# Retention by 64x64 blocks on quarters of TensorE's array, with decays as powers of the position and the state summed in PSUM

## The chip, the cores and the metric

The kernel runs on one core of a Trainium2 chip. The metric is the time of one execution on the device, in microseconds; lower is better. TensorE multiplies matrices and writes its sums to PSUM, VectorE (DVE), ScalarE (ACT) and GpSimd (POOL) do elementwise work, and SyncE (SP) issues the transfers between device memory and the on-chip memory SBUF. Each engine works through its own queue in order.

## The reference

For each of 8 batch rows and 8 heads, retention over 576 positions with head size 64, then two feed-forward layers over all 4608 tokens. Everything is in 32-bit floats.

```python
scores = (1 / sqrt(64)) * (q @ k.T)                     # per head, 576 x 576
ret = scores * where(i >= j, gamma[h] ** (i - j), 0)    # gamma[h] = 1 - 2 ** (-5 - h)
x = (ret @ v)                                           # heads side by side: 4608 x 512
x = square(relu(x @ moe_w_in)) @ moe_w_out              # 512 -> 2048 -> 512
y = elu(x @ moe2_w_in) @ moe2_w_out                     # 512 -> 2048 -> 512
```

## The kernel before

Tokens are cut into 9 blocks of 512 (`TB`). The first projection of the first layer (`up`, L393-403) goes block by block and, within a block, over 16 slices `f` of 128 features: per slice 12 matmuls of 512 columns, since weights and activations are each split into a high and a low half and three of the four products are kept. `act` (L414) applies relu and square on ScalarE and stores the result to device memory (`gd`). The other three projections follow later (from about 567 us) with seven products of a Strassen scheme in place of eight; `up_product` and `Down.multiply` (L570, L722) are their matmuls. The change does not touch them except for `m_tile`, which says in which of two pools a tile of theirs lies.

Retention makes the activations of the first projection. It is done in 40 chunks (`CHUNKS`): every batch row has four chunks of 128 positions and one of 64, the short one last in even batch rows and first in odd ones, so that no chunk crosses a block. For chunk `c`, with `s` its first position and `n` its length, and head pairs `p` (4) of heads `e` (2):

- `a_load` (L292) loads q and k with the head dimension on partitions, and k and v with positions on partitions.
- `a_scores` (L304): k times q, one matmul per head with 64 rows of the array, 128 columns of output positions.
- `a_decay` (L315): VectorE multiplies the scores by a table of scaled decays, zero above the diagonal.
- `a_qscale` and `a_kscale` (L324, L330): q and k are scaled by powers of gamma; on VectorE inside the loop, on GpSimd at the start.
- `a_out` (L337): the running state times the scaled q (one matmul per head pair, since the state holds two heads as diagonal blocks of a 128x128 matrix), plus v times the decayed scores, summed in one PSUM tile `o`.
- `a_evac` (L353): ScalarE copies `o` to `xraw`.
- `a_state` (L363): VectorE scales the state by a power of gamma, TensorE forms k times v in PSUM (`d`), VectorE adds it to the state.

Four chunks are worked off at the start, for block 0. The chunks of block n+1 are inserted between the slices of block n: a table `at` gives the steps, and at such a step `second(c)` (output, copy-out, state) and `first(c+1)` (scores, scalings, decay of the next) are issued just before the 12 matmuls of the slice; the loads of chunk c+2 are issued right after. `x_split` near the end of a block splits the finished activations into halves.

Two further strands run beside. In block 0, `Converter` turns the weights from 64-bit to 32-bit floats (`join` on VectorE) and splits them (`Half`), one half-slice per step. From block 1 on, `factor_steps` (L250) prepares the weight factors of the later Strassen products: 48 `Factors`, each with three steps spread over the loop: load of raw weights, conversion, sums on VectorE (L225), and a split in two (`split`, L227): ScalarE writes the high half to a tile of its own, GpSimd writes the low half in place; `store` (L237) writes each with one transfer to device memory (`wd`), the previous factor's at the start of the next. High and low halves use a ring of five tiles (`turn`). The order inside the first block is left to the tile framework's order of issue; later it is written out.

Of the kernel before, what the change touches and what calls it, by code (L numbers as in the profile page):

```python
# [51 lines left out]
C_D, C_Q, C_G, C_K = 0, 1024, 1536, 1544  # L52
C_W = 1664
# [3 lines left out]

def constants():
# [4 lines left out]
    i = np.arange(128)  # L63
    rel = i[None, :] - i[:, None]
    for h in range(H):
        p, e = divmod(h, 2)
        dec = np.where(rel >= 0, scale * gamma[h] ** np.maximum(rel, 0), 0.0)
        t[:, C_D + (e * NP + p) * 128:][:, :128] = dec
        t[64 * e:64 * e + 64, C_Q + p * 128:C_Q + p * 128 + 128] = scale * gamma[h] ** i
        t[64 * e:64 * e + 64, C_G + p] = gamma[h] ** 128  # L70
        t[64 * e:64 * e + 64, C_G + NP + p] = gamma[h] ** 64
        t[:, C_K + h] = gamma[h] ** (128 - i)
        t[:64, C_K + H + h] = gamma[h] ** (64 - i[:64])
    return t.astype(np.float32)
# [3 lines left out]
def retention_moe_moe(ctx, tc, qk_full, qk_half, kv, w1, w2, cst, out):  # L78
# [107 lines left out]
    turns = [0]  # L186

    def turn(shape, dtype, name):
        n = turns[0] % 5
        turns[0] += 1  # L190
        if n > 2:
            return place(23 + n, shape, dtype, name)
        return mpool.tile(shape, dtype, tag=f"turn{n}", name=name)

    class Factors:
# [13 lines left out]
        def start(self):  # L209
            self.r = turn([128, 8, 128], F32, "qr")  # L210
# [16 lines left out]
        def split(self):  # L227
# [3 lines left out]
            h = turn([128, 7, 128], F32R, "qh")  # L231
            nc.scalar.activation(out=h, in_=r, func=ACTF.Copy)  # L232
# [40 lines left out]
    decay = cs[:, C_D:C_D + 1024].rearrange("p (e q i) -> p e q i", e=2, q=NP)  # L273
    qdec = cs[:, C_Q:C_Q + 512].rearrange("p (q i) -> p q i", q=NP)
# [88 lines left out]
    def a_state(c, eng):  # L363
        b, s, n = CHUNKS[c]
        kv_c = kv_t.pop(c)
        if s + n == S:
            return
# [605 lines left out]
```

## Time and profile before

| | |
|---|---|
| median of 3 runs | 1636.27 us (1635.28 to 1638.92) |
| profiled execution | 1638.09 us, its span 1636.0 us |
| mean granted TensorE clock | 0.992 |
| first projection begins | 33.55 us after the span's start |
| later stages begin | about 567 us |
| TensorE busy | 1599.3 us (98%) |
| VectorE, ScalarE, GpSimd busy | 1247.2, 883.5, 133.0 us |
| moved by DMA | 379 MB |

The profile is of one execution. A group's line gives the line of the kernel, the engine, the operation, the tiles written and read, their shapes, how many there were, the busy time in us and the mean length of one in ns, and then how long the engine stood idle before them and what ended that. Matmuls overlap, so their lengths are not their cost; the distance from start to start is. TensorE's weight loads have rows of their own (PEld). "DMA share" is the share of the time in which the 16 DMA engines worked, and "PEclk" the share of the full clock that TensorE was granted.

### The profile page before, as it was taken

The numbers are of one execution on the slowest core, as the hardware profiler recorded it, in microseconds if no ns is written. First come the engines' busy times: TensorE is split into PE (matmuls) and PEld (weight loads), VectorE is DVE, ScalarE is ACT, GpSimd is POOL, SyncE is SP. The second block draws the span as 40 slices with busy tenths as digits, with TensorE's granted clock in tenths as the row PEclk, the third lists the DMA queues.
The fourth block names the chain that finished last, engine by engine and source line by source line (L and its number), as shares of the span: only waits on it lengthen the run. The fifth ranks groups of instructions, "written<-read, shape, count | busy, mean of one in ns | idle before, by whom it ended". The sixth has DMA issues, their size and how long they took to land. (4 is left out here: it accounts for less than half of the span.)

```text
span 1636.0 us, 25789 instructions
## 1 busy us (share of the span) xinstructions
PE 1599.3 (98%) x9832; PEld 1497.8 (92%) x9832; DVE 1247.2 (76%) x1580; ACT 883.5 (54%) x1207; POOL 133.0 (8%) x75
## 2 busy tenths in 40 slices
PE   7999999999999999999999999999999999999998
PEld 6887787787888899999999999999999899999998
DVE  7948667676757188899889688888888877776875
ACT  3555455455556544554454577777777544444443
POOL 3312222222222000000000000000000000000000
PEclk8999999999999999999999999999999999999999
DMA  7869999889988993653577984644658864345241
GB/s 253 270 188 317 304 286 309 278 266 327 305 283 270 317 379 137 249 200 135 206 247 244 343 311 181 215 182 153 222 202 307 329 237 134 98 155 163 89 136 39
DMA packets 230683, 378.99 MB, mean 232 GB/s; under 512 B 15776, under 2 KB 169376, under 8 KB 230560
## 3 DMA queue, kind: packets, MB, share of 16 engines
q1 hardware_dynamic: 230560, 377.35, 68.4%
q8 instruction: 77, 1.26, 0.3%
q14 instruction: 46, 0.38, 0.1%
HBM read 220.00 MB, written 157.29 MB: 231 GB/s over the span
## 5 line engine op out<-in xcount | busy, mean ns | idle before, releaser
L703 ACT ACTIVATE gh<-gq 128x768 fp32r<-128x768 f32 x336 | 284.7, 848 | 371.4 <-PE w L722 150.8
L709 DVE TENSOR_TENSOR gl<-gq,gh 128x768 fp32r<-128x768 f32 x336 | 316.8, 954 | 147.4 <-ACT gh L703 147.3
L722 PE MATMUL w<-gh,wf 128*128 128x384 f32 x1152 | 292.5, 334 | 0.0
L399 PE MATMUL h<-xp,w 128*128 128x512 f32 x576 | 230.8, 401 | 2.5 <-ACT r L418 1.7
L401 PE MATMUL h<-xp,w 128*128 128x512 f32 x576 | 226.3, 393 | 3.4 <-DVE xp L388 3.4
L400 PE MATMUL h<-xp,w 128*128 128x512 f32 x576 | 226.4, 393 | 0.0
L722 PEld LDWEIGHTS w<-gh,wf 128*128 128x128 f32 x1152 | 208.1, 188 | 0.0
L722 PE MATMUL a<-gh,wf 128*128 128x384 f32 x768 | 195.0, 334 | 1.5 <-ACT gh L703 1.5
L722 PE MATMUL e<-gh,wf 128*128 128x384 f32 x768 | 195.1, 334 | 0.0
L722 PE MATMUL w<-gl,wf 128*128 128x384 f32 x576 | 192.8, 335 | 0.2 <-DVE gl L709 0.2
L694 DVE TENSOR_TENSOR gq<-gq 128x1536 f32<-128x1536 f32 x96 | 168.5, 1755 | 1.7
L570 PE MATMUL w<-xc,wf 128*128 128x384 f32 x864 | 161.4, 334 | 0.0
L570 PEld LDWEIGHTS w<-xc,wf 128*128 128x128 f32 x864 | 150.8, 188 | 0.0
L722 PEld LDWEIGHTS a<-gh,wf 128*128 128x128 f32 x768 | 138.6, 188 | 1.9 <-ACT gh L703 1.8
L722 PEld LDWEIGHTS e<-gh,wf 128*128 128x128 f32 x768 | 138.8, 188 | 0.0
L399 PEld LDWEIGHTS h<-xp,w 128*128 128x128 f32 x576 | 109.5, 190 | 29.2 <-ACT r L418 2.2
L401 PEld LDWEIGHTS h<-xp,w 128*128 128x128 f32 x576 | 109.0, 189 | 28.7 <-DVE xp L388 5.1
L234 POOL TENSOR_TENSOR qr<-qr,qh 128x896 fp32r<-128x896 f32 x48 | 102.3, 2131 | 347.1 <-ACT qh L232 259.4
L722 PE MATMUL a<-gl,wf 128*128 128x384 f32 x384 | 128.5, 335 | 1.7 <-DVE gl L709 1.7
L722 PE MATMUL e<-gl,wf 128*128 128x384 f32 x384 | 129.4, 337 | 0.0
L400 PEld LDWEIGHTS h<-xp,w 128*128 128x128 f32 x576 | 109.4, 190 | 21.8
L418 ACT ACTIVATE r<-h 128x512 f32<-128x512 f32 x144 | 84.9, 590 | 77.6 <-PE h L401 77.1
(81 smaller groups left out, 2337.1 us busy)
## 6 DMA issues: line engine op xcount, KB each, us to landing
gq<-gd SPq DMA_DIRECT2D x96, 768.0 KB, 5.8
wf<-wd SPq DMA_DIRECT2D x84, 512.0 KB, 6.6
gd<-h SPq DMA_DIRECT2D x96, 384.0 KB, 3.3
qraw<-w SPq DMA_DIRECT2D x96, 256.0 KB, 4.8
xc<-x2d SPq DMA_DIRECT2D x30, 768.0 KB, 6.6
wd<-qh SPq DMA_DIRECT2D x48, 448.0 KB, 4.8
wd<-qr SPq DMA_DIRECT2D x48, 448.0 KB, 5.0
gd<-g SPq DMA_DIRECT2D x96, 192.0 KB, 3.6
```

What stands on the lines that cost most here:

```text
L234: nc.gpsimd.tensor_tensor(out=rl, in0=r, in1=h.bitcast(F32), op=ALU.subtract)
L399: nc.tensor.matmul(out=h, lhsT=w[:, 0, k, :], rhs=x[k][:, 0, :], start=(k == 0), stop=False)
L400: nc.tensor.matmul(out=h, lhsT=w[:, 1, k, :], rhs=x[k][:, 0, :], start=False, stop=False)
L401: nc.tensor.matmul(out=h, lhsT=w[:, 0, k, :], rhs=x[k][:, 1, :], start=False, stop=(k == KC - 1))
L418: nc.scalar.activation(out=r, in_=h, func=ACTF.Relu)
L570: nc.tensor.matmul(out=t[:, jj, :TP], lhsT=w[:, jj, c, a, :], rhs=x[:, b, c, :], start=(i in FRESH and c == 0 and n == 0), stop=(c == 1 an ...
L694: nc.vector.tensor_tensor(out=gq[out, h], in0=gq[x, h], in1=gq[y, h], op=op)
L703: nc.scalar.activation(out=gh, in_=src, func=ACTF.Copy)
L709: nc.vector.tensor_tensor(out=gl, in0=src, in1=gh.bitcast(F32), op=ALU.subtract)
L722: nc.tensor.matmul(out=t[:, c, :TP], lhsT=w[:, jj, c, a, :], rhs=parts[b][:, jj, :], start=(i in FRESH and q == 0 and jj == 0 and m == 0), ...
```

## The change

gamma^(i-j) is written as gamma^(i-256) times gamma^(256-j), with positions counted in the batch row. v is multiplied by the second factor once (`a_vscale`, VectorE; GpSimd for the later chunks at the start), and the finished output by the first, in the copy-out (`a_evac`), which moves from ScalarE to VectorE. So scores need only a mask of ones and zeros, q and k are not scaled, and k times v needs no decay: its sum over the chunks of a batch row stays in one PSUM tile (`d_t`), and ScalarE copies that to `state` after each chunk (`a_state`).

Scores are computed for 64x64 blocks, with 64 rows and 64 columns of the array to each matmul, and the block above the diagonal is left out. Heads of odd pairs have their position halves swapped on partitions. State times q, per head, also takes a quarter of the array, for which half of the heads of q are loaded a second time on the other partitions (`q2`). p times v takes quarters for the first 64 output positions and all 128 rows for the second 64; the next chunk's scores are issued between these two (`insert`). Chunks are loaded three ahead in place of two, k one later than the rest. The large table `fall` of position powers is loaded whole at the start. `o` has one buffer of two banks.

In `Factors`, the raw tile `qr` has two fixed places, and both halves go into one tile `hl`, alternating by 128 elements, with two buffers; one transfer stores both. `m_tile` puts tile 5 into the second pool.

```diff
-C_D, C_Q, C_G, C_K = 0, 1024, 1536, 1544
-C_W = 1664
+C_M, C_V, C_G = 0, 192, 272
+C_W = C_G + KC * S
...
+    mask = np.ones((2, 64, 3, 64))
+    mask[0, :, 0], mask[1, :, 0], mask[1, :, 1], mask[0, :, 2] = (causal,) * 4
...
+            t[:, C_V + H * c + h] = gamma[h] ** (256 - (s + j))
...
+            t[64 * half:64 * half + 64, C_G + S * k:C_G + S * k + S] = \
+                scale * gamma[2 * p + e] ** (np.arange(S) - 256)
...
-            self.r = turn([128, 8, 128], F32, "qr")
+            self.r = place(26 + self.n % 2, [128, 8, 128], F32, "qr")
...
-            h = turn([128, 7, 128], F32R, "qh")
-            nc.scalar.activation(out=h, in_=r, func=ACTF.Copy)
-            rl = self.r.bitcast(F32R)[:, at:at + 7, :]
-            nc.gpsimd.tensor_tensor(out=rl, in0=r, in1=h.bitcast(F32), op=ALU.subtract)
-            self.halves = (h.bitcast(F32), rl.bitcast(F32))
+            self.hl = mpool.tile([128, 7, 2, 128], F32R, tag="hl", name="hl", bufs=2)
+            nc.scalar.activation(out=self.hl[:, :, 0, :], in_=r, func=ACTF.Copy)
+            nc.gpsimd.tensor_tensor(out=self.hl[:, :, 1, :], in0=r,
+                                    in1=self.hl[:, :, 0, :].bitcast(F32), op=ALU.subtract)
...
-            for n, half in enumerate(self.halves):
-                nc.sync.dma_start(out=wd[self.layer, part][:, :, q, jj, c, n, :], in_=half)
+            nc.sync.dma_start(out=wd[self.layer, part][:, :, q, jj, c, :, :], in_=self.hl.bitcast(F32))
...
+    mask = cs[:, C_M:C_M + 192].rearrange("p (g i) -> p g i", g=3)
+    grow = cs[:, C_V:C_V + 10 * H].rearrange("p (c h) -> p c h", c=10)
+    fall = cs[:, C_G:].rearrange("p (w e t) -> p w e t", w=2, e=2)
+    state = apool.tile([128, 2, 2, D], F32, name="state")
...
-        t = apool.tile([128, 2, NP, n], F32, tag="qk", name="qk", bufs=2)
+        if c % 3:
+            t = place(23 + c % 3, [128, 2, NP, n], F32, "qk")
+        else:
...
-        t = apool.tile([128, 2, H, D], F32, tag="kv", name="kv", bufs=2)
-        nc.sync.dma_start(out=t[:n], in_=kv[b * S + s:b * S + s + n])
-        kv_t[c] = t
+        if s:
+            q2_t[c] = ring.tile([128, 2, n], F32, tag=f"t{2 + c % 3}", name="q2")
+            src = q2_full[FULL.index(c)] if n == 128 else q2_half[HALF.index(c)]
+            nc.sync.dma_start(out=q2_t[c], in_=src)
+        if c % 3:
+            v = apool.tile([128, H, D], F32, tag="v", name="v", bufs=2)
+        else:
+            v = ring.tile([128, H, D], F32, tag="t5", name="v")
+        nc.sync.dma_start(out=v, in_=kv[c, :, 1])
+        v_t[c] = v
+
+    def k_load(c):
+
+        b, s, n = CHUNKS[c]
+        if s + n < S:
+            k_t[c] = apool.tile([128, H, D], F32, tag="k", name="k", bufs=2)
+            nc.sync.dma_start(out=k_t[c], in_=kv[c, :, 0])
+
...
-        for p in range(NP):
-            for e, sc in enumerate(sc_t[c]):
-                r = slice(64 * e, 64 * e + 64)
-                nc.tensor.matmul(out=sc[:n, p, :n], lhsT=qk[r, 1, p, :], rhs=qk[r, 0, p, :],
-                                 start=True, stop=True)
+        for pp in range(2):
+            for half in range(n // 64):
+                for p in range(2 * pp, 2 * pp + 2):
+                    for e, sc in enumerate(sc_t[c]):
+                        r = slice(64 * e, 64 * e + 64)
+                        to = slice(64 * ((half + p) % 2), 64 * ((half + p) % 2) + 64)
+                        k = qk[r, 1, p, 64 * half:64 * half + 64]
+                        if half == 0 and p % 2 == 0:
+                            q, out = qk[r, 0, p, :], sc[to, pp, :n // 64, :]
+                        elif half == 0 and n == 128:
+                            q = qk[r, 0, p, :].rearrange("p (g i) -> p g i", g=2)
+                            out = sc[to, pp, 0:3:2, :]
+                        else:
+                            q = qk[r, 0, p, 64 * half:64 * half + 64]
+                            out = sc[to, pp, half * (1 + p % 2), :]
+                        nc.tensor.matmul(out=out, lhsT=k, rhs=q, start=True, stop=True)
...
-            pt = apool.tile([128, NP, 128], F32, tag=f"p{e}", name=f"p{e}")
-            nc.vector.tensor_tensor(out=pt[:n, :, :n], in0=sc[:n, :, :n],
-                                    in1=decay[:n, e, :, :n], op=ALU.mult)
+            pt = ring.tile([128, 2, 3, 64], F32, tag=f"t{e}", name="p")
+            nc.vector.tensor_tensor(out=pt[:, :, :g, :], in0=sc[:, :, :g, :],
+                                    in1=mask[:, :g, :].unsqueeze(1).to_broadcast([128, 2, g, 64]),
+                                    op=ALU.mult)
...
+    def a_vscale(c, eng):
+        v = v_t[c]
+        eng.tensor_tensor(out=v, in0=v, in1=grow[:, c % 10].unsqueeze(2).to_broadcast([128, H, D]),
+                          op=ALU.mult)
+
...
+        o = ps.tile([128, 2, 4, 128], F32, tag="o", name="o")
+        v = v_t[c]
+        pts = p_t.pop(c)
+        rows = [slice(64 * w, 64 * w + 64) for w in range(2)]
+        begun = set()
+
+        def add(p, e, at, lhsT, rhs):
+            w, to = p % 2, p // 2
+            nc.tensor.matmul(out=o[rows[to], w, e, at], lhsT=lhsT, rhs=rhs,
+                             start=(w, to) not in begun, stop=False, skip_group_check=True)
+            begun.add((w, to))
+
+        heads = [(p, e) for e in range(2) for p in range(NP)]
+            for p, e in heads:
+                r = rows[p % 2]
+                q = qk_t[c][r, 0, p, :] if e == p % 2 else q2_t[c][r, p // 2, :]
+                add(p, e, slice(0, n), state[r, p // 2, e, :], q)
+        for p, e in heads:
+            r = rows[p % 2]
+            add(p, e, slice(0, 64), v[r, 2 * p + e, :], pts[e][r, p // 2, 0, :])
+        if between:
+            between()
+        if n == 128:
+            for p, e in ((p, e) for e in range(2) for p in (0, 2, 1, 3)):
+                add(p, e, slice(64, 128), v[:, 2 * p + e, :], pts[e][:, p // 2, 1 + p % 2, :])
...
+            if s == 0:
+                d_t[0] = ps.tile([128, 2, 2, D], F32, tag="d", name="d")
+            for p, e in heads:
+                nc.tensor.matmul(out=d_t[0][rows[p % 2], p // 2, e, :], lhsT=k_t[c][:, 2 * p + e, :],
+                                 rhs=v[:, 2 * p + e, :], start=(s == 0 and p < 2 and e == 0),
+                                 stop=False, skip_group_check=True)
...
-        nc.scalar.copy(out=xraw[g // TB][:, :, cols], in_=o[:, :, :n])
+        nc.vector.tensor_tensor(out=xraw[g // TB].rearrange("p (w e) t -> p w e t", w=2)[:, :, :, cols],
+                                in0=o[:, :, :2, :n], in1=fall[:, :, :, s:s + n], op=ALU.mult)
...
-        if s + n == S:
-            return
-        if s:
-            eng.tensor_tensor(out=state, in0=state,
-                              in1=sdec[n].unsqueeze(2).to_broadcast([128, NP, 128]), op=ALU.mult)
...
+        if s + n < S:
+            nc.scalar.copy(out=state, in_=d_t[0])
...
+            if loaded[0]:
+                k_load(loaded[0] - 1)
...
+    def insert(c):
+
+        more = c + 1 < len(CHUNKS)
+        o = a_out(c, (lambda: a_scores(c + 1, ("s0", "s1"))) if more else None)
+        a_evac(c, o)
+        a_state(c)
+        if more:
+            a_vscale(c + 1, nc.vector)
+            a_decay(c + 1)
+        later.append(lambda: load_to(c + 3))
...
-    nc.sync.dma_start(out=cs[:, :C_Q], in_=cst[:, :C_Q])
+    nc.sync.dma_start(out=cs[:, :C_G], in_=cst[:, :C_G])
     load_to(1)
-    nc.sync.dma_start(out=cs[:, C_Q:], in_=cst[:, C_Q:])
-
-
-    warm = ps.tile([128, NP, 128], F32, tag="r", name="warm", bufs=3)
+    nc.sync.dma_start(out=cs[:, C_G:], in_=cst[:, C_G:])
...
+    zero = ring_tile(5, F32, "zero").rearrange("p a n -> p (a n)")
+    nc.vector.memset(zero, 0.0)
+    warm = ps.tile([128, TB], F32, tag="w", name="warm", bufs=3)
     for _ in range(4):
-        nc.tensor.matmul(out=warm, lhsT=state[:, 0, :], rhs=state, start=True, stop=True)
+        nc.tensor.matmul(out=warm, lhsT=zero[:, :128], rhs=zero[:, :TB], start=True, stop=True)
...
+    load_to(2)
...
-        a_state(c, nc.vector)
-        load_to(c + 2)
+        a_state(c)
+        a_evac(c, o)
+        load_to(c + 3)
-        a_evac(c, o)
...
-        return pools[n // 6].tile([128, 2, 2, TP], dtype, tag=f"m{n}", name=name)
+        return pools[n // 5].tile([128, 2, 2, TP], dtype, tag=f"m{n}", name=name)
...
-            at[step] = [(second, c)] + ([(first, c + 1)] if c + 1 < len(CHUNKS) else [])
+            at[step] = [(insert, c)]
...
+        "qk_half": chunks(qk, HALF),
+        "q2_full": chunks(q2, FULL),
+        "q2_half": chunks(q2, HALF),
+        "kv": np.stack([np.stack([rows(k, c), rows(v, c)], 1) for c in range(len(CHUNKS))]),
+        "w1": weights(moe_w_in[order], moe_w_out),
```

More of the change, by code (lines that the diff above doesn't have):

```diff
@@ L62, in constants, with retention_moe_moe @@
     t = np.zeros((128, C_W), np.float64)
[L63 to L73, printed above, removed]
+    r = np.arange(128)
+    causal = (np.arange(64)[None, :] >= r[:64, None]).astype(np.float64)
+    mask = np.ones((2, 64, 3, 64))
+    mask[0, :, 0], mask[1, :, 0], mask[1, :, 1], mask[0, :, 2] = (causal,) * 4
+    t[:, C_M:C_M + 192] = mask.reshape(128, 192)
+    for c, (b, s, n) in enumerate(CHUNKS[:10]):
+        for h in range(H):
+            j = r % 64 if n == 64 else (r + 64) % 128 if swapped(h) else r
+            t[:, C_V + H * c + h] = gamma[h] ** (256 - (s + j))
+    for p in range(NP):
+        for e in range(2):
+            k, half = place_of(p, e)
+            t[64 * half:64 * half + 64, C_G + S * k:C_G + S * k + S] = \
+                scale * gamma[2 * p + e] ** (np.arange(S) - 256)
     return t.astype(np.float32)
 @with_exitstack
-def retention_moe_moe(ctx, tc, qk_full, qk_half, kv, w1, w2, cst, out):
+def retention_moe_moe(ctx, tc, qk_full, qk_half, q2_full, q2_half, kv, w1, w2, cst, out):
     nc = tc.nc
@@ L185, in retention_moe_moe @@
     RAW = (20, 21, 22, 23)
[L186 to L193, printed above, removed]
     class Factors:
@@ L272, in retention_moe_moe @@
     cs = apool.tile([128, C_W], F32, name="cs")
[L273 to L279 removed]
+    mask = cs[:, C_M:C_M + 192].rearrange("p (g i) -> p g i", g=3)
+    grow = cs[:, C_V:C_V + 10 * H].rearrange("p (c h) -> p c h", c=10)
+    fall = cs[:, C_G:].rearrange("p (w e t) -> p w e t", w=2, e=2)
+    state = apool.tile([128, 2, 2, D], F32, name="state")
+    qk_t, q2_t, k_t, v_t, p_t = {}, {}, {}, {}, {}
     xraw = {}
@@ L361, in a_evac, with a_state @@
             nc.vector.tensor_tensor(out=t[:, :, 1], in0=raw, in1=t[:, :, 0].bitcast(F32), op=ALU.subtract)
[L363 removed]
+    def a_state(c):
         b, s, n = CHUNKS[c]
[L365 to L383 removed]
+        if s + n < S:
+            nc.scalar.copy(out=state, in_=d_t[0])
     def x_split(n, k):
@@ L428, in retention_moe_moe @@
                     for j in range(NB)]
-    nc.vector.memset(state, 0.0)
     loaded = [0]
@@ L934, in _layout, with chunks, rows @@
     qk = np.stack([pairs(q), pairs(k)], 2)
-    def chunks(ids):
-        return np.stack([qk[CHUNKS[c][0], :, :, :, CHUNKS[c][1]:CHUNKS[c][1] + CHUNKS[c][2]] for c in ids])
-    def rows(a):
-        return a.transpose(0, 2, 1, 3).reshape(NT, H, D)
+    q2 = qk[:, :, 0].reshape(B, 2, 64, NP // 2, 2, S)
+    q2 = np.stack([q2[:, 1, :, :, 0], q2[:, 0, :, :, 1]], 1).reshape(B, 128, NP // 2, S)
+    def chunks(a, ids):
+        return np.stack([a[CHUNKS[c][0], ..., CHUNKS[c][1]:CHUNKS[c][1] + CHUNKS[c][2]] for c in ids])
+    def rows(a, c):
+        b, s, n = CHUNKS[c]
+        t = a[b, :, s:s + n].transpose(1, 0, 2)
+        out = np.zeros((128, H, D), a.dtype)
+        for h in range(H):
+            if n == 128:
+                out[:, h] = np.roll(t[:, h], 64, 0) if swapped(h) else t[:, h]
+            else:
+                out[64 * swapped(h):64 * swapped(h) + 64, h] = t[:, h]
+        return out
+    heads = np.empty((KC, 2), np.int64)
+    for p in range(NP):
+        for e in range(2):
+            heads[place_of(p, e)] = 2 * p + e
+    order = (heads.reshape(-1, 1) * D + np.arange(D)).reshape(-1)
     def weights(w_in, w_out):
@@ L947, in _layout @@
     return {
-        "qk_full": chunks(FULL),
-        "qk_half": chunks(HALF),
-        "kv": np.stack([rows(k), rows(v)], 1),
-        "w1": weights(moe_w_in, moe_w_out),
+        "qk_full": chunks(qk, FULL),
+        "qk_half": chunks(qk, HALF),
[3 more added lines that the diff above has]
+        "w1": weights(moe_w_in[order], moe_w_out),
         "w2": weights(moe2_w_in, moe2_w_out),
```

71 lines of the change are left out of this document (17 added, 54 removed).

## The prediction

> **What bounds the kernel now.** I read the page's busy table first, then the windows by stage, then the timeline of one insertion of retention, then the waits.
>
> ```profile
> PE 1599.3 (98%) x9832; PEld 1497.8 (92%) x9832; DVE 1247.2 (76%) x1580; ACT 883.5 (54%) x1207; POOL 133.0 (8%) x75
> ```
>
> ```profile
> 0.00:33.50 33.50, 25.08 (x240) 19.03 (x240) 23.06 (x36) 10.75 (x17) 11.48 (x14) 0.85 0.73 269
> 33.50:97.00 63.50, 61.79 (x449) 51.54 (x450) 54.28 (x89) 35.03 (x64) 19.23 (x14) 0.97 0.71 231
> 97.00:523.00 426.00, 411.87 (x2903) 343.61 (x2902) 293.76 (x570) 227.72 (x375) 98.03 (x46) 0.99 0.93 290
> 345.00:403.00 58.00, 57.70 (x395) 48.10 (x394) 42.38 (x82) 31.99 (x53) 15.03 (x7) 1.00 1.00 314
> 567.00:1636.00 1069.00, 1056.61 (x6049) 1047.17 (x6048) 867.67 (x869) 586.12 (x714) 0.00 (x0) 1.00 0.58 204
> ```
>
> The columns after the length are PE, PEld, DVE, ACT, POOL busy, then granted clock, DMA share, GB/s. TensorE sets the pace everywhere. The change lives in the first 523 us: the start (33.5 us), token block 0 (63.5 us), token blocks 1 to 7 (426 us). There TensorE is never long idle, and the DMA engines are nearly full too: 0.93 on average, 1.00 from 345 to 403 us, where TensorE nevertheless ran 57.70 of 58 us. The 1069 us behind are untouched but for the pool that holds one tile.
>
> One insertion of a full chunk in the middle of a batch row, from the timeline of TensorE (start, length, operation, count):
>
> ```profile
> 141.34 0.39 PE L401 MATMUL h<-xp,w 128*128 128x512 f32 x1
> 141.57 1.05 PE L342 MATMUL o<-qk,state 128*128 128x128 f32 x8
> 142.55 1.09 PE L347 MATMUL o<-p,kv 128*64 128x128 f32 x16
> 143.48 0.63 PE L375 MATMUL d<-kv 128*64 128x64 f32 x16
> 144.04 1.16 PE L312 MATMUL sc<-qk 64*128 64x128 f32 x16
> 145.13 0.50 PE L399 MATMUL h<-xp,w 128*128 128x512 f32 x1
> 145.47 0.39 PE L400 MATMUL h<-xp,w 128*128 128x512 f32 x1
> ```
>
> The profile shows every call of these as two passes (the 4 state calls as 8). From 141.57 to 145.13 is 3.56 us, and the first projection matmul starts its successor 0.34 us later instead of 0.23, so an insertion costs 3.67 us. It lies bare on the path.
>
> ```profile
> L342 PE MATMUL o<-qk,state 128*128 128x128 f32 x224 | 30.9, 282 | 7.1 <-DVE state L381 3.1 <-DVE qk L328 2.4 <-DVE state L383 1.4
> L347 PE MATMUL o<-p,kv 128*64 128x128 f32 x512 | 38.9, 289 | 0.8 <-DVE p L320 0.5
> L375 PE MATMUL d<-kv 128*64 128x64 f32 x448 | 20.6, 232 | 0.0
> L312 PE MATMUL sc<-qk 64*128 64x128 f32 x512 | 37.3, 286 | 9.0 <-DMA qk<-qk_full 9.0
> L312 PE MATMUL sc<-qk 64*64 64x64 f32 x128 | 6.7, 245 | 0.1
> ```
>
> These are counts and durations. A full-array pass of 128 columns follows the last after (1.05 - 0.282) / 7 = 0.11 us. Sixteen half-array passes (128\*64 or 64\*128) take about what eight full ones take, so two halves run at once, whether the array is cut by columns or by rows. For 64 columns a pair takes (0.63 - 0.232) / 7 = 0.057 us. I call these slots: 0.111 and 0.057 us. The insertion above is 24 slots of 0.111 and 8 of 0.057, 3.12 us; the other 0.55 us are three changes of array shape.
>
> **The passes.** Before, over all 40 chunks: state 224 x 0.111 and 32 passes on half chunks at about 0.105, 28.2 us; p times v 512/2 x 0.111 + 128/2 x 0.057 = 32.1; k times v 512/2 x 0.057 = 14.6; scores 32.1. Sum 107.0 us.
>
> After, if four quarters run at once: state needs 16 quarter passes per chunk in place of 8 full ones, 4 slots: 28 x 4 x 0.111 + 4 x 4 x 0.057 = 13.3 us. p times v is split: the first 64 columns in quarters, 40 x 4 x 0.057 = 9.1; the second 64 with all 128 rows, 32 x 8 x 0.057 = 14.6. k times v stays 14.6. Scores leave the block above the diagonal out and have 16 calls per full chunk, 32 x (4 x 0.111 + 4 x 0.057) + 8 x 4 x 0.057 = 23.3. Sum 74.9, so 32.1 us less. An insertion still changes shape three times (quarters, halves, whole), so the 0.55 us stay: the example goes from 3.67 to 2.81 us. That the next chunk's scores stand between the two parts of p times v keeps the quarters together.
>
> No row shows four quarters at once. The bounds: four at a time (-32.1), or two at a time as in the rows above. Then state is 28 x 8 x 0.111 + 4 x 8 x 0.057 = 26.7, the split product 18.2 + 14.6, k times v 14.6, scores 32 x (8 x 0.111 + 8 x 0.057) + 8 x 8 x 0.057 = 46.7, together 120.8, 13.8 us more. I take four: rows and columns each already give independent halves. 31 of the 40 chunks are inserted in blocks 1 to 7 and 5 in block 0: -25 and -4 us.
>
> **The waits on the insertion.**
>
> ```profile
> PE sc L312 <- DMA qk<-qk_full: 6.5, 4, 2.5
> PE h L401 <- DVE xp L388: 3.4, 4, 1.5
> PE h L399 <- ACT r L418: 1.7, 1, 1.7
> PE o L342 <- DVE qk L328: 1.4, 1, 1.4
> ```
>
> That is TensorE's own list for 97 to 523 us (total, times, longest). Loading three chunks ahead in place of two gives each load one insertion more, 426 / 31 = 13.7 us, against a longest wait of 2.5: -6.5. The q scaling is gone: -1.4. The other two wait on chains through VectorE and ScalarE. VectorE's work per chunk is told by these:
>
> ```profile
> L320 DVE TENSOR_TENSOR p<-sc,cs 128x512 f32<-128x512 f32 x64 | 41.2, 686 | 9.1 <-PE sc L312 7.5 <-PE o L347 1.0
> L328 DVE TENSOR_TENSOR qk<-qk,cs 128x512 f32<-128x512 f32 x25 | 30.9, 1238 | 4.1 <-PE sc L312 3.6
> L334 DVE TENSOR_TENSOR kv<-kv,cs 128x512 f32<-128x512 f32 x24 | 22.2, 924 | 0.0
> L369 DVE TENSOR_TENSOR state<-state,cs 128x512 f32<-128x512 f32 x24 | 16.5, 686 | 0.0
> L381 DVE TENSOR_TENSOR state<-d,state 64x256 f32<-64x256 f32 x48 | 20.2, 421 | 4.2 <-PE d L375 1.9
> L320 DVE TENSOR_TENSOR p<-sc,cs 64x256 f32<-64x256 f32 x16 | 6.1, 409 | 0.1
> ```
>
> Now 2 x 0.69 + 1.24 + 0.92 + 0.69 + 2 x 0.42 = 5.1 us; after, the masks 2 x 0.55 (384 elements, between 409 and 686 ns), the v scaling 0.92 and the copy-out with its factor 0.69, 2.7 us. VectorE loses 2.4 us per insertion, but it was not the bound, so I count half of the 5.1 us of the two other waits, -2.5, and -2 of the 4 us that the clock of 0.99 costs over 426 us (it falls after stalls). Block 0 gets -3.5: 1.9 for its clock of 0.97, 1.6 for waits of the same kinds.
>
> New waits: the copy-out now waits at the head of VectorE's queue for p times v, with the next masks and the factor steps behind it, as the state additions did for k times v. The state copy waits at the head of ScalarE's queue, with relu of the next slice behind it, whose matmuls follow it on TensorE anyway. One output tile in PSUM in place of three means that the next insertion waits for the copy-out, 13.7 us old by then. These I cost at nothing; without that distance, at the start, each is about 1 us. SyncE issues two loads more per chunk and one store fewer per factor, about even.
>
> **DMA.** In blocks 1 to 7 the engines have 0.93 x 426 = 396 us of work. q2 adds 128 KB per chunk, 3.8 MB; the last chunk of each batch row no longer loads k, the half chunks load 128 rows; about +3 MB net, or at 290 / 0.93 = 312 GB/s +10 us.
>
> ```profile
> wd<-qh SPq DMA_DIRECT2D x46, 448.0 KB, 4.8
> wd<-qr SPq DMA_DIRECT2D x46, 448.0 KB, 5.1
> ```
>
> These 42 MB of factor halves go in runs of 512 bytes now, and of 1 KB after. With larger packets the last stage moves 204 / 0.58 = 352 GB/s, so the gain lies between 0 and 42/0.312 - 42/0.352 = 15 us; I take 7. That leaves 399 us of DMA work against a TensorE that would need 426 - 25 - 6.5 - 1.4 - 2.5 - 2 = 389. I take DMA as the floor of these blocks: 399, a gain of 27 where TensorE alone would give 37.
>
> **The start.**
>
> ```profile
> 19.08 1.16 PE L312 MATMUL sc<-qk 64*128 64x128 f32 x16 [1.79 <-DMA qk<-qk_full]
> 33.55 0.80 PE L399 MATMUL h<-xp,w 128*128 128x512 f32 x1 [0.47 <-ACT xp L360]
> ```
>
> Ahead of the first raw weights stand 2880 KB of loads now, and 4360 KB after (the large decay table, q2 and all of chunk 2), 1.5 MB or 5.6 us at 269 GB/s. Conversion starts that much later; VectorE has less to do and the 1.79 us wait goes. Bounds -4 and +6; I take +2.
>
> **Sum.** -27 (blocks 1 to 7), -7.5 (block 0: 4 and 3.5), +2: -32.5 us. The profiled execution took 1638.1 us around a span of 1636.0; that gives 1605.6. It lay 1.8 us above the median of the three runs shown, 1636.3, so on that footing 1604.
>
> **The rivals.**
>
> *Issue-bound quarters.* In the densest row, k times v, a pair of passes every 57 ns is one per 29 ns; four quarters at 64 columns want one per 14. For it: nothing in the trace is denser. Against: passes run in pairs there, so the array, not the issue, may have set 29. At 29 ns: state 14.8, split product 18.6 + 14.6, k times v 14.6, scores 33.4, sum 96.0, only 11 us less; blocks 1 to 7 then need 426 - 8.5 - 12.4 = 405, block 0 gains 5: 1638.1 - 21 - 5 + 2 = 1614, or 1612 against the median.
>
> The Trainium skill, "TensorE: Matmul & The Clock Gate", section "Wait — 56ns, not 53.3ns?", has such a floor: starts of small matmuls come no closer than about 25 ns. By it the sum of passes would be some 89 us and the time, an estimate, about 1607. The 29 ns row agrees with it but doesn't reach it.
>
> *Two quarters at a time.* +13.8 us of passes, +10.7 in blocks 1 to 7 against -12.4 of waits, +2 in block 0 against -3.5, +2 at the start: within 2 us of 1636, no change. For it: only pairs are seen. Against: both cuts work singly.
>
> *DMA is no floor.* Shares over 0.93 hold with TensorE undisturbed (the 345:403 row). Then blocks 1 to 7 reach 389, 10 us more: 1594.
>
> *Slower: the factor stores.* The halves now share one tile with two buffers, and one store waits for ScalarE and GpSimd both.
>
> ```profile
> ACT qh L232 <- DMA wd<-qr: 7.5, 3, 2.8
> ```
>
> A factor comes every 426 / 46 = 9.3 us; its store is issued a third into the next, and ScalarE may write the buffer again in the middle of the one after, some 12 us later. The halves land in 4.8 and 5.1 us. If 896 KB behind a full ring took 13, ScalarE would stand 1 us on each factor with relu behind it, then TensorE: +46 us, 1650. Below 12 us it costs nothing; from about 12.7 us the gain is gone. Against: the buffer that it replaces was also waited for two factors on, and that cost 7.5 us in three places.
>
> **How the numbers follow.** Forecast 0.48 (1604, its own range 1597 to 1612), issue-bound 0.20 (1612), two at a time 0.12 (1635), DMA no floor 0.12 (1594), slower 0.08 (1650). About 0.2% (3.3 us) is what a measurement of this kernel tells from no change. The first, second and fourth are faster, as is a third of the two-at-a-time case: 0.84. The rest of that case is split between no change (0.05) and slower, which with the stores makes 0.11. The range reaches from 1588 (start at its best, DMA no floor) to 1630 (two at a time in some of the passes).
>
> **What would show it.** Four quarters: 16 state passes of 64\*64 in about half a microsecond and an inserted full chunk of about 2.8 us. Pairs: 0.9 us for them, and over 4 us. Issue-bound: 64-column quarter passes at an even spacing of 25 to 29 ns in place of bursts of four. The waits: no scores waiting for qk, no state waiting for VectorE. The DMA floor: a share near 1.0 in blocks 1 to 7, over about 400 us, with ScalarE or VectorE waiting for qraw, g or the factor stores in place of qk. The start: the first projection matmul near 35.5 us. Wrong altogether would be a stage of 426 us or more in blocks 1 to 7, or a change in the last 1069 us.

## The result, and the profile after

| | before | after |
|---|---|---|
| median | 1636.92 us (1635.28 to 1638.92, 4 runs) | 1600.98 us (1600.70 to 1601.64, 4 runs) |
| profiled execution | 1638.09 us, span 1636.0 | 1600.95 us, span 1599.2 |
| mean granted clock | 0.992 | 0.994 |

The ratio is 0.978, with a 95% interval of 0.9764 to 0.9797: faster. All medians here are of fast runs; one run with loads two ahead (3129.85 us) and one with the halves side by side (5565.93 us) count as slow and are left out. Between the profiled executions the span fell by 36.8 us.

The profile page's busy table of the changed kernel:

```profile
PE 1564.3 (98%) x11112; PEld 1460.6 (91%) x11112; DVE 1180.5 (74%) x1512; ACT 873.9 (55%) x1199; POOL 127.0 (8%) x71
```

TensorE has 1280 passes more and 35 us less to do. The windows by stage (length; PE, PEld, DVE, ACT, POOL busy; granted clock, DMA share, GB/s), cut where the start, block 0, blocks 1 to 7 and the later stages begin:

```profile
0.00:34.50 34.50, 22.77 (x418) 16.88 (x418) 17.57 (x32) 8.62 (x15) 6.04 (x9) 0.91 0.86 297
34.50:94.00 59.50, 57.06 (x567) 46.43 (x567) 49.37 (x78) 36.57 (x65) 18.54 (x14) 0.97 0.81 266
94.00:487.00 393.00, 384.25 (x3889) 313.99 (x3888) 236.51 (x516) 218.35 (x367) 98.12 (x46) 0.99 0.96 319
531.00:1599.00 1068.00, 1056.24 (x6048) 1046.83 (x6046) 867.21 (x869) 586.06 (x714) 0.00 (x0) 1.00 0.58 204
```

By the starts of the first projection matmul of each block, to two places: the start is 1.0 us longer (33.55 to 34.51), block 0 is 3.8 us shorter (63.3 to 59.5), blocks 1 to 7 are 33.5 us shorter (426.6 to 393.2), block 8 without retention takes 43.5 us in both, and what follows differs by half a microsecond. So the gain lies in blocks 1 to 7. I parted their time further by the starts of successive projection matmuls, which are 0.227 us apart when nothing intervenes: the gaps with retention in them exceed that by 107.5 us before and by 71.5 after (-36.0), all other gaps by 14.0 before and 16.6 after (+2.5).

One insertion of a full chunk, from TensorE's timeline (start, length):

```profile
133.99 0.39 PE L437 MATMUL h<-xp,w 128*128 128x512 f32 x1
134.31 0.32 PE L376 MATMUL o<-qk,state 64*64 64x128 f32 x1
134.31 0.32 PE L376 MATMUL o<-q,state 64*64 64x128 f32 x1
134.32 0.32 PE L376 MATMUL o<-qk,state 64*64 64x128 f32 x1
134.33 0.32 PE L376 MATMUL o<-q,state 64*64 64x128 f32 x1
...
134.79 0.41 PE L376 MATMUL o<-p,v 64*64 64x64 f32 x16
135.03 0.85 PE L346 MATMUL sc<-qk 64*64 64x128 f32 x32
135.81 0.69 PE L376 MATMUL o<-p,v 128*64 128x64 f32 x16
136.32 0.64 PE L398 MATMUL d<-v,k 128*64 128x64 f32 x16
136.89 0.50 PE L435 MATMUL h<-xp,w 128*128 128x512 f32 x1
137.22 0.40 PE L436 MATMUL h<-xp,w 128*128 128x512 f32 x1
```

From 133.99 to 136.89 is 2.90 us, 2.67 beyond the projection's own 0.227, and the successor comes 0.33 us later, another 0.11: 2.78 us where the same reckoning gave 3.67 before. Sixteen state passes of 128 columns start within 134.31 to 134.79, and the sixteen quarter passes of 64 columns of p times v take 0.24 us from their first start to the first start of the scores.

What waits in blocks 1 to 7, from the lists of TensorE and of ScalarE (total, times, longest):

```profile
PE h L437 <- DVE xp L424: 3.3, 4, 1.5
PE h L435 <- ACT xp L423: 2.9, 2, 2.6
PE h L435 <- ACT r L454: 1.4, 1, 1.4
...
ACT hl L237 <- DVE qr L230: 108.6, 42, 4.4
ACT g L455 <- DMA gd<-g: 25.1, 21, 2.9
```

No scores wait for q and k any more. TensorE's remaining waits are on the splits of its own activations (`xp`) and on relu. ScalarE's wait for the stores of `g` has grown: the tile that square writes has three buffers, and the store of the one wanted next is still under way. Before, in its blocks 1 to 7, this wait was short:

```profile
ACT g L419 <- DMA gd<-g: 3.0, 2, 2.0
```

### The profile page after: what moved, and what is told of

Read it like the earlier page. It is cut to its first block, busy times and chain, and to the rows that moved or that the text cites. A ratio compares the mean times of both kernels' runs of the same rounds, so it can differ in the third digit from the quotient of the medians.

```text
span 1599.2 us, 28168 instructions
## 1 busy us (share of the span) xinstructions
PE 1564.3 (98%) x11112; PEld 1460.6 (91%) x11112; DVE 1180.5 (74%) x1512; ACT 873.9 (55%) x1199; POOL 127.0 (8%) x71
## 5 line engine op out<-in xcount | busy, mean ns | idle before, releaser
L128 DVE TENSOR_SCALAR qr<-qr 128x512 f32<-128x512 f32 x48 | 24.9, 518 | 145.7 <-ACT qr L140 145.7
L238 POOL TENSOR_TENSOR hl<-qr,hl 128x896 fp32r<-128x896 f32 x48 | 102.4, 2133 | 312.8 <-ACT hl L237 233.3
```

The costliest lines, as they stand in the source:

```text
L128: nc.vector.tensor_scalar(out=m, in0=m, scalar1=2.0, scalar2=W_MAX, op0=ALU.max, op1=ALU.min)
L238: nc.gpsimd.tensor_tensor(out=self.hl[:, :, 1, :], in0=r, in1=self.hl[:, :, 0, :].bitcast(F32), op=ALU.subtract)
```

## The experiments

All ratios are to the kernel before, in the same comparison. The changed kernel itself was timed in the first comparison alone; the median of the kernel before moved between 1635.0 and 1636.9 us from one comparison to the next, so a difference of some 2 us from the changed kernel can't be told from none. Six kernels are the changed one with an edit that tests a step, three are the kernel before with a part of the change, and three look for a better version.

**The factor halves in two tiles again.** This undoes one part: two stores per factor with runs of 512 bytes in place of one with runs of 1 KB.

```diff
-            self.hl = mpool.tile([128, 7, 2, 128], F32R, tag="hl", name="hl", bufs=2)
+            h = mpool.tile([128, 7, 128], F32R, tag="hh", name="hh", bufs=2)
+            l = mpool.tile([128, 7, 128], F32R, tag="hw", name="hw", bufs=2)
...
-            nc.sync.dma_start(out=wd[self.layer, part][:, :, q, jj, c, :, :], in_=self.hl.bitcast(F32))
+            for n, half in enumerate(self.halves):
+                nc.sync.dma_start(out=wd[self.layer, part][:, :, q, jj, c, n, :], in_=half)
```

> The changed kernel with the factor halves in two tiles again and stored by two transfers in runs of 512 bytes; all else as changed. If the DMA engines are the floor of token blocks 1 to 7 (share 0.96 of 393 us in the changed kernel), 42 MB in runs half as long cost 5 to 15 us: 1606 to 1616 us. If TensorE sets the pace and the transfers only fill the time beside it, the time stays within 2 us of 1601 and the DMA share rises to about 0.99.

Measured: 1614.6 us, ratio 0.9866 (0.985 to 0.9882), 13.6 us above the changed kernel. The window of its blocks 1 to 7:

```profile
94.00:498.00 404.00, 387.45 (x3890) 315.15 (x3890) 235.95 (x515) 217.09 (x366) 98.05 (x46) 0.99 0.99 311
```

And from its ScalarE's waits in them:

```profile
ACT g L457 <- DMA gd<-g: 46.7, 26, 5.5
```

The bytes are the same (311 x 404 and 319 x 393 are both 125 MB), but the engines work 0.99 x 404 = 400 us in place of 0.96 x 393 = 377. The stage is now as long as that work, and the waits on stores of `g` rise from 25.1 to 46.7 us. Here DMA is the floor.

**The same data in two stores of 1-KB runs.** The run before changed two things, the length of the runs and the number of transfers. This one changes only the number.

```diff
-            nc.sync.dma_start(out=wd[self.layer, part][:, :, q, jj, c, :, :], in_=self.hl.bitcast(F32))
+            for i in (slice(0, 4), slice(4, 7)):
+                nc.sync.dma_start(out=wd[self.layer, part][:, i, q, jj, c, :, :],
+                                  in_=self.hl[:, i].bitcast(F32))
```

> The changed kernel with each factor stored by two transfers in place of one, but with the same runs of 1 KB (four products, then three). The run with the halves apart lost 13.6 us. If the length of the runs was the cause, this one stays within 2 us of 1601. If the cause was the second transfer on SyncE's queue (46 more of about 0.6 us each, 26 us, ahead of the stores that ScalarE waits for), it loses 8 to 14 us too: 1609 to 1615 us.

Measured: 1603.22 us, ratio 0.98 (0.9785 to 0.9815); DMA share 0.95 over 396 us, 376 us of work. So most of the 13.6 us above come from the length of the runs; the second transfer accounts for some 2 us, which is within the noise.

**Loads two chunks ahead.**

```diff
-        later.append(lambda: load_to(c + 3))
+        later.append(lambda: load_to(c + 2))
```

> The changed kernel with chunks loaded two ahead in the loop, as before the change, in place of three. If the waits of the scores on q and k went because of the earlier load, they come back, about 6.5 us in blocks 1 to 7 as before the change, or more, since the scores now stand in front of the second half of p times v: 1606 to 1612 us. If they went for another reason (shorter queues), the time stays at 1601.

Measured: 1625.05 us, ratio 0.9932 (0.9911 to 0.9953): 24 us lost, far more than the 6.5 us of waits that loading three ahead was meant to remove. TensorE's waits in blocks 1 to 7:

```profile
PE sc L346 <- DMA qk<-qk_full: 10.0, 6, 3.5
PE d L398 <- DMA k<-kv: 6.0, 8, 1.4
PE sc L346 <- DMA qk<-qk_half: 2.0, 2, 1.7
```

The window of block 4, of this kernel and then of the changed one:

```profile
268.90:337.40 68.50, 60.96 (x578) 49.21 (x577) 33.22 (x78) 30.41 (x51) 13.24 (x7) 0.90 0.83 273
```

```profile
259.60:317.60 58.00, 55.49 (x578) 45.01 (x577) 34.94 (x82) 31.77 (x55) 13.73 (x7) 1.00 1.00 330
```

The changed kernel loads k one chunk later than the rest; with two ahead that is one ahead, and eight times k times v waits for k, a wait the kernel before didn't have. TensorE's waits on loads come to 18 us, and the clock falls with the stalls: to 0.90 in block 4, which is about 6.9 us of its 68.5 (a tenth).

**The order of quarters.** Heads of one quarter follow each other in place of going round the four.

```diff
+        by_quarter = [(p, e) for p in range(NP) for e in range(2)]
...
-            for p, e in heads:
+            for p, e in by_quarter:
...
-        for p, e in heads:
+        for p, e in by_quarter:
```

> The changed kernel with the two heads of a quarter next to each other in state times q and in the first part of p times v, so that four passes in a row go to the same quarter. If TensorE starts passes strictly in the order written, the quarters then work almost one after the other: 13 slots in place of 4, +1.0 us for the state and +0.5 us for p times v on a full chunk, about +45 us in all, 1645 us. If each quarter works off its own passes independently, the order inside a group of sixteen doesn't matter and the time stays at 1601.

Measured: 1602.0 us, ratio 0.979 (0.9769 to 0.981): no difference from the changed kernel. TensorE's timeline where p times v ends and the scores begin:

```profile
135.54 0.45 PE L376 MATMUL o<-p,v 64*64 64x64 f32 x14
135.77 0.27 PE L346 MATMUL sc<-qk 64*64 64x128 f32 x1
135.78 0.23 PE L376 MATMUL o<-p,v 64*64 64x64 f32 x2
135.82 0.86 PE L346 MATMUL sc<-qk 64*64 64x128 f32 x31
```

A pass of the scores starts ahead of two passes of p times v that were issued before it. The quarters don't wait for each other's turn, and the order in the code costs some 0.05 us per insertion (9.99 in place of 9.78 us in the four insertions of a block). The Trainium skill, "TensorEngine Tiling (Array Packing)", section "Key Properties", says that tiles operate independently; this trace agrees.

**The three parts on the kernel before.** Halves side by side alone; three chunks ahead alone, with third buffers for q, k and v; both. The decayed scores move to the ring where the halves need their room. Cores of the edits:

```diff
-            h = turn([128, 7, 128], F32R, "qh")
+            self.hl = mpool.tile([128, 7, 2, 128], F32R, tag="hl", name="hl", bufs=2)
...
-            for n, half in enumerate(self.halves):
-                nc.sync.dma_start(out=wd[self.layer, part][:, :, q, jj, c, n, :], in_=half)
+            nc.sync.dma_start(out=wd[self.layer, part][:, :, q, jj, c, :, :], in_=self.hl.bitcast(F32))
```

```diff
+        if c % 3 == 2:
+            t = place(24, [128, 2, NP, n], F32, "qk")
+        else:
+            t = apool.tile([128, 2, NP, n], F32, tag="qk", name="qk", bufs=2)
...
-        later.append(lambda: load_to(c + 2))
+        later.append(lambda: load_to(c + 3))
```

> The kernel before with nothing changed but the factor halves side by side in one tile, stored by one transfer (the two tiles of decayed scores lie in the ring, and one tile of the late stages in the second pool, to make room). If the DMA engines hold the slower kernel back as they do the changed one, it gains the same 13 us: about 1623 us. If TensorE's own work still hid most of the transfers there (share 0.93 of a stage longer by 33 us), it gains 2 to 6 us: 1631 to 1635 us.

> The kernel before with nothing changed but chunks loaded three ahead in the loop, with a third buffer for q and k and for k and v. By the waits in the profile of before (6.5 us of scores waiting for q and k in blocks 1 to 7, and some of the slower clock after them) it gains 6 to 10 us: 1627 to 1631 us. By the run that loads two ahead in the changed kernel, which lost 25 us, it gains 20 or more: under 1617 us.

> The kernel before with both of these, halves side by side and three ahead, but retention as it was. What is left to the changed kernel's 1601 us is the quarters and the decays moved to the positions. If each part gives its own share, 36 us less the 10 to 14 of these two, about 1623 us, and the quarters are worth some 22 us net. If loads and stores were the whole matter, 1605 us or less, and the quarters nothing.

| on the kernel before | median | ratio (interval) |
|---|---|---|
| halves side by side | 1634.32 us | 0.9986 (0.9974 to 0.9997) |
| three ahead | 1629.66 us | 0.9963 (0.9953 to 0.9973) |
| both | 1628.9 us | 0.9956 (0.9942 to 0.9971) |

Blocks 1 to 7 of the first of these, and of the one with both:

```profile
96.00:522.00 426.00, 413.85 (x2926) 345.23 (x2926) 300.33 (x574) 231.04 (x380) 98.15 (x46) 1.00 0.88 293
```

```profile
94.00:512.00 418.00, 409.58 (x2912) 341.28 (x2911) 298.79 (x570) 228.42 (x377) 98.22 (x46) 1.00 0.88 293
```

The halves take DMA from 0.93 x 426 = 396 us of work to 375, and the stage stays at 426: in the kernel before, DMA was not the bound. Quarters, decays and the sum in PSUM bring the other 28 us (1628.9 to 1601.0). The parts don't add up: the halves are worth 2 us to the kernel before and 13.6 to the changed one, and the third chunk ahead 7 and 24. For the halves the shorter TensorE work is the reason: 396 us of DMA work fit beside the 426 us of the stage before; the 400 of the changed kernel with runs of 512 bytes don't fit beside the 381 us that its best version below takes. The two figures for loading ahead are not of quite the same step, since the changed kernel loads k one chunk later and issues the scores earlier in an insertion.

**More work for VectorE.** Three operations per inserted chunk that leave v as it is (the larger of v and v), behind the v scaling and ahead of the masks.

```diff
             a_vscale(c + 1, nc.vector)
+            for _ in range(3):
+                v = v_t[c + 1]
+                nc.vector.tensor_tensor(out=v, in0=v, in1=v, op=ALU.max)
             a_decay(c + 1)
```

> The changed kernel with three more passes of VectorE over the scaled v of each inserted chunk (the maximum of v with itself, 512 elements per partition, which leaves v as it is): 2.1 to 2.8 us of VectorE per chunk, about what the change took off it. If VectorE's relief was worth what the prediction gave it (2.5 us in blocks 1 to 7), 1601 to 1604 us. If its chain to ScalarE and so to TensorE set the pace, 1608 us or more.

Measured: 1647.17 us, ratio 1.0077 (1.0056 to 1.0098), 46 us above the changed kernel and slower than the one before. The added operations in the groups of its blocks 1 to 7:

```profile
L487 DVE TENSOR_TENSOR v<-v 128x512 f32<-128x512 f32 x90 | 101.1, 1123 | 3.1
```

TensorE's longest wait there, and the window:

```profile
PE o L376 <- DVE p L354: 20.4, 14, 3.2
```

```profile
94.00:530.00 436.00, 401.63 (x3905) 325.40 (x3904) 335.58 (x605) 221.21 (x371) 99.57 (x46) 0.97 0.87 289
```

The additions cost 3.4 us per chunk (101.1 / 30), more than the change took off VectorE (2.4 us by the prediction; by the busy times of blocks 1 to 7, 293.8 and 236.5 us for 31 chunks, 1.8 in the mean), so the run isn't that step undone; they lie ahead of the masks too, where the kernel before had no such load. TensorE waits 20.4 us for masks, which it hardly does in the changed kernel (0.3 us in these blocks), and loses clock (0.97). VectorE, busy for only 236.5 of 393 us, has little room to spare at this place of its queue.

Part of the cost is not VectorE's own work. One by one in the trace, 69 of the 90 additions take 691 to 694 ns. The other 21 take 2470 to 2572 ns, and just these start while GpSimd is at work on the low half of a factor; each ends about 0.55 us after GpSimd does. From the timelines of the two engines, the three additions of one chunk:

```profile
139.60 0.68 DVE L361 TENSOR_TENSOR v<-v,cs 128x512 f32<-128x512 f32 x1
140.20 2.13 POOL L238 TENSOR_TENSOR hl<-qr,hl 128x896 fp32r<-128x896 f32 x1 [5.18 <-ACT hl L237]
140.32 4.02 DVE L487 TENSOR_TENSOR v<-v 128x512 f32<-128x512 f32 x3
```

At 0.69 us each the three would cost 2.1 us per chunk; the rest, 1.3, is this waiting for GpSimd.

**The split of activations ahead of the factor step.** In the changed kernel, the first slice of a block can wait for the activations' split on ScalarE (`xp`), which stands behind the high half of a factor in ScalarE's queue. The timeline of the changed kernel at 374 us:

```profile
373.56 1.02 DVE L230 TENSOR_TENSOR qr<-qr 128x128 f32<-128x128 f32 x4
374.62 0.95 ACT L237 ACTIVATE hl<-qr 128x896 fp32r<-128x896 f32 x1 [3.46 <-DVE qr L230]
375.47 1.13 ACT L423 ACTIVATE xp<-xraw 128x512 fp32r<-128x512 f32 x2
375.70 2.09 POOL L238 TENSOR_TENSOR hl<-qr,hl 128x896 fp32r<-128x896 f32 x1 [7.60 <-ACT hl L237]
376.12 2.82 DVE L424 TENSOR_TENSOR xp<-xraw,xp 128x512 fp32r<-128x512 f32 x2 [1.53 <-ACT xp L423]
376.14 0.72 PE L435 MATMUL h<-xp,w 128*128 128x512 f32 x1 [2.58 <-ACT xp L423]
...
378.39 0.79 PE L437 MATMUL h<-xp,w 128*128 128x512 f32 x1 [1.11 <-DVE xp L424]
```

ScalarE stood 3.46 us idle, at the head of its queue a copy that waited for VectorE's sums, behind it the split that TensorE wanted. The same copy sets off GpSimd's low half of the factor, and VectorE's part of the activations' split starts beside it: the first of the two takes 2.22 us in place of 0.68, and TensorE waits another 1.11 us. The edit moves the split ahead:

```diff
-        while factors_done < min(3 * len(factors), -(-3 * len(factors) * (step + 1 - FROM) // (TO - FROM))):
-            next(factor_step)
-            factors_done += 1
-        for fn, c in at.get(step, ()):
-            fn(c)
...
                 x_split(n + 1, k)
+        while factors_done < min(3 * len(factors), -(-3 * len(factors) * (step + 1 - FROM) // (TO - FROM))):
+            next(factor_step)
+            factors_done += 1
+        for fn, c in at.get(step, ()):
+            fn(c)
```

> The changed kernel with the split of the next block's activations issued ahead of the factor step of the same slice instead of behind it. In the changed kernel TensorE loses 8 to 9 us at the first slices of blocks 2, 3, 5 and 6 (with the slower clock that follows one of them), waiting for the low half of the activations, whose high half stood behind a factor's high half on ScalarE. If that order is the cause, 1592 to 1596 us. If the DMA engines are the floor of these blocks, the gain is given back as waits on raw weights or stores: 1599 to 1602 us.

Measured: 1600.59 us, ratio 0.979 (0.9767 to 0.9814): no change. TensorE's list of waits over blocks 1 to 7 has one line:

```profile
PE h L435 <- ACT r L454: 7.2, 5, 2.8
```

The waits on `xp` are gone (6.2 us), and no split takes longer than 1.11 us, where six took 2.2; but 7.2 us of waiting for relu are there in place of 1.4. ScalarE waits for the stores of `g` no less than before (28.7 us against 25.1). That this is what holds up its relu is argued from the order of its queue; the next run bears on it.

**Both: the split first, and a fourth buffer for `g`.** The edit above, and

```diff
-        g = mpool.tile([128, TB], F32, tag="g", name="g", bufs=3)
+        g = mpool.tile([128, TB], F32, tag="g", name="g", bufs=4)
```

> The changed kernel with the activations' split ahead of the factor step, as in an earlier run that gave nothing back in total, and a fourth buffer for the squared output g, whose store ScalarE waited for there (29.6 us in 23 places). If those waits are short lateness of stores behind a full queue, a buffer more takes most of them: 1592 to 1597 us. If the DMA engines' total is the floor, the waits move elsewhere and the time stays at 1599 to 1602 us.

Measured: **1591.27 us (1590.0 to 1592.72, 5 runs), ratio 0.9733 (0.9718 to 0.9749)**, the fastest of all. TensorE's list of waits over blocks 1 to 7, whole:

```profile
PE o L376 <- DVE xraw L409: 0.7, 1, 0.7
PE h L435 <- ACT r L454: 0.3, 1, 0.3
PE o L376 <- DVE p L354: 0.3, 1, 0.3
```

And their window:

```profile
94.30:475.70 381.40, 380.00 (x3890) 313.02 (x3889) 229.27 (x516) 218.17 (x366) 97.62 (x46) 1.00 0.98 329
```

ScalarE's wait for the stores of `g` before it writes `g` is off the list, the clock is 1.00, and TensorE is busy for 380.0 of 381.4 us with 374 us of DMA work beside it. The insertions are as long as before the edit, 71.5 us; the other gaps fall from 16.6 to 4.8. Against the changed kernel that is 9.7 us by the medians and 8 by the ratios. The fourth buffer wasn't tried alone.

**The factor steps spread to the end of block 8.** Block 8 has no insertions; with 122 slices to spread the factors over in place of 114, there is less of their DMA per block.

```diff
-    FROM, TO = KF + 2, steps - KF + 4
+    FROM, TO = KF + 2, steps - 4
```

> The changed kernel with the 144 factor steps spread over 122 slices in place of 114, so that 7% of the factors' loads and stores (about 4.5 MB, 14 us of work for the DMA engines) leave blocks 1 to 7 for block 8. If the DMA engines hold blocks 1 to 7 (share 0.96), they get 4 to 8 us shorter: 1593 to 1597 us. If the stalls there come from the order on ScalarE alone, nothing changes beyond 2 us; if block 8 pays for it (share 0.94 there), 1601 or more.

> Both together: split first, four buffers for g, and the factors spread over 122 slices. If order and DMA each hide the other's gain, the sum is more than the parts: 1586 to 1592 us, near TensorE's own need. If not, no better than the better of the two.

Measured: alone 1599.06 us, ratio 0.9779 (0.9762 to 0.9796); together with the two edits above 1594.18 us, ratio 0.975 (0.9734 to 0.9767), 3 us above those without it. The combination against them in the later stages:

```profile
518.30:1591.00 1072.70, 1058.81 (x6049) 1046.85 (x6048) 868.36 (x870) 587.11 (x716) 0.00 (x0) 1.00 0.58 206
```

```profile
519.30:1588.00 1068.70, 1057.29 (x6049) 1048.56 (x6047) 867.57 (x869) 586.15 (x714) 0.00 (x0) 1.00 0.58 204
```

Its blocks 1 to 7 take the same 381.3 us, though with 0.95 x 381 = 362 us of DMA work: once TensorE no longer waits, less DMA brings nothing there. Behind block 8 it takes 4 us more. The spread alone does shorten blocks 1 to 7, from 393.2 to 385.9 us, with ScalarE's waits for stores of `g` down from 25.1 to 9.4; what comes behind block 8 takes 6 us more there (1075.0) and gives it back. What of the late factors that is, these runs don't show.

## Why the prediction was right, and where its steps were off

The forecast was 32.5 us less than the profiled execution, 1604 against the median; the profiled execution became 37.1 us shorter and the median 1601.0. Both the direction and most of the mechanism held; one term was far too small, and two were counted that hardly came (VectorE's relief, and the waits and clock of block 0).

**The passes: right.** Four quarters at once: the example insertion was to take 2.81 us and takes 2.78. In blocks without a wait in their insertions the four gaps go from 12.9 to 9.8 us, and the five of block 6 from 14.7 to 10.3: 4 x 3.1 + 3 x 4.4 = 26 us for the seven blocks, where I had 25. Neither rival on the quarters is left. Two at a time would have made the insertion longer than before. Issue-bound quarters at 29 ns would need 0.46 us for the sixteen passes of p times v, and they take 0.24, that is 15 ns each; their starts come in groups of four within 20 ns, the groups 57 ns apart, the slot of the prediction. The floor of about 25 ns between starts in the Trainium skill, "TensorE: Matmul & The Clock Gate", section "Wait — 56ns, not 53.3ns?", would give, counted for each pass, an estimated 0.40 us. The trace disagrees with it for passes that go to different quarters: their starts are 6 to 7 ns apart.

**The waits on the insertion: right for the loads, wrong for VectorE.** Insertions lost 36.0 us; beside the 26 of the passes, 7.9 are the scores' wait and the q scaling, both gone as priced, which leaves 2. That these are the 2 us for the clock is not shown: block 4, at 0.95 before, is at 1.00, but block 6, at 1.00 before, is at 0.94, and the stage's mean stays at 0.99. The -2.5 us for VectorE's relief didn't come: projection matmuls wait 3.3 us for VectorE's split where they waited 3.4, and all gaps without retention together grew by 2.5. Those waits were not a matter of VectorE's load. In both kernels 2.6 us of them lie behind splits that started beside GpSimd's work on a factor and took 2.2 us in place of 0.68 (three splits before, two after); with the split issued ahead of the factor's copy they were gone, at the same load. Nor does "not the bound" mean that VectorE has room: 3.4 us more per chunk ahead of the masks cost 46. The price of 1.24 us for scaling q had the same origin: beside GpSimd it took up to 2.2 us, elsewhere 0.69.

**DMA: the term that was mis-sized.** I took 399 us of work as the floor of blocks 1 to 7 and so gave back 10 of the 37 us that TensorE gained. The work was 377, 374 in the best version. The mis-sized term is the gain of longer runs: 7 us taken, 15 the upper bound, 23 measured (400 with runs of 512 bytes, 377 with 1 KB) and 21 on the kernel before (396 to 375). The rest of the difference is the added traffic: 10 us taken, some 4 measured (396 before, 400 with all of the change but the longer runs). My bound took the gain from the mean rates of two stages with different mixes of transfers, 312 and 352 GB/s, which say little of these stores alone. The floor as a mechanism is real: with 512-byte runs the stage takes 404 us for 400 us of work, close to 406, which is my reckoning (396 + 10) without a gain. So the rival "DMA is no floor" was the nearer one for these blocks (389 forecast, 393 measured), but for another reason than it gave: the floor dropped below TensorE. That 399 was only 6 us off is partly luck, since the 10 us given back to a floor that didn't hold stand where some 12 us of other waits came.

What took 393 rather than 381 us I had no price for: a wait for a buffer of `g`, named only as a sign of the DMA floor, whose stores land late while the DMA engines are nearly full, and a split that stood behind a factor's copy. Moving the split alone gained nothing; with the fourth buffer it gave 8 to 10 us. How much the fourth buffer would give by itself is open.

**Block 0 and the start: the sizes were off, against each other.** Block 0 gained 3.8 us where I had 7.5. Its insertions gave 3.3 (17.2 to 13.9) against 4, and the 3.5 us for waits and clock gave 0.5: its clock is 0.97 as before. The start cost 1.0 us against 2. The 1.8 us wait of the scores went as forecast. But a copy of the state, for which I had about 1 us, kept TensorE waiting for 3.4; it stood behind a split of weights in ScalarE's queue. The longest wait in TensorE's list up to 94 us is a new one, and not a loss of that size: it is the 4.6 us from the span's start to the first load, which the warm-up matmuls used to fill. They now come later, and the first scores start at 4.55 us in place of 7.67. The list begins:

```profile
PE sc L346 <- DMA qk<-qk_full: 4.6, 1, 4.6
PE d L398 <- ACT state L419: 3.4, 1, 3.4
```

**The factor stores: not seen.** This slower rival needed a store of 896 KB that takes 13 us to land. It takes 5.9, and ScalarE waits for none of them in blocks 1 to 7:

```profile
wd<-hl SPq DMA_DIRECT2D x48, 896.0 KB, 5.9
```

The errors partly cancel, which is luck: 6.5 too little in blocks 1 to 7 and 1 at the start, 3.7 too much in block 0.

## What to carry to other kernels

When an edit takes work off the engine that sets the pace, ask for each load, store and buffer beside it how much later it may be now; a part that is worth little by itself can be worth far more once the stage is shorter (here 2 and 14 us for the run length). Price a wait by what stands ahead of it in its engine's queue, not by that engine's busy share; look at what runs beside it too, since a mean length can hide two quite different ones; and when taking one wait away moves nothing, look for the one that stands right behind it and take both. A DMA share close to 1 is a floor only if the work, share times length, stays the same after the change: the length of the runs moves it as surely as the bytes do.

## What was not expected of the hardware

- Quarter passes of 64 columns start 6 to 7 ns apart in groups of four, 15 ns each over all, and a pass to one quarter can start ahead of earlier ones to another.
- Runs of 512 bytes in place of 1 KB, for 42 MB, cost 21 and 23 us of the 16 DMA engines' time (396 and 375 us on the kernel before, 400 and 377 on the changed one), in a stage that moves 125 MB.
- A VectorE operation on two SBUF inputs of 512 elements per partition that starts while GpSimd subtracts one SBUF tile from another ends about 0.55 us after GpSimd does. The additions with a mean of 1123 ns are 69 of 691 to 694 ns and 21 of 2470 to 2572, the latter all begun during GpSimd's operation. A small broadcast table as second input is no protection: the scaling of k in the kernel before took 2.6 us in the three cases that began so. The scaling of v (0.68 us in all 30) began before GpSimd's operation wherever the two met.
